# An attention and two-MoE kernel on one core: MoE1's weight differences move from GpSimd to VectorE, each one slot behind its cast, and the first pass of the experts is put in another order

## The chip, the cores and the metric

The kernel runs on one core of a Trainium2 chip, alone. The metric is the device time of one execution in microseconds. Five engines take part: TensorE (PE; its weight loads are shown apart as PEld), VectorE (DVE), ScalarE (ACT), GpSimd (POOL) and SyncE (SP, which here only issues DMAs). Every engine runs its own instructions strictly in order and waits for others through semaphores.

## What is computed

```python
def _moe_ref(x, w_in, w_out):                       # MoE1, dense
    h = x @ w_in                                    # 896x768 @ 768x2048
    g = h * (1.0 / (1.0 + np.exp(-1.702 * h)))
    return (g @ w_out).astype(np.float32)           # 896x2048 @ 2048x768

def _moe2_ref(x, w_gate, w_output_gate, w1, w2):    # MoE2, 8 experts, one per token
    logits = x @ w_gate
    e_idx = np.argmax(logits, axis=1)
    ...                                             # probs = softmax(logits)
    gate_w = probs[np.arange(N), e_idx]
    eom = 1.0 / (1.0 + np.exp(-(x @ w_output_gate)))
    for e in range(E):
        mask = e_idx == e
        h = np.maximum(x[mask] @ w1[e], 0.0)        # 768 -> 1024
        ye = h @ w2[e]                              # 1024 -> 768
        out[mask] = gate_w[mask, None] * eom[mask, e, None] * ye

def reference(**kwargs):
    attn_out = _attn_ref(**attn_kwargs)             # causal attention, 2 x 12 heads x 448 x 64
    x = attn_out.transpose(0, 2, 1, 3).reshape(896, 768)
    return _moe2_ref(x=_moe_ref(x=x, **moe_kwargs), **moe2_kwargs)
```

MoE1's two weight matrices arrive as float64, all else as float32.

## The kernel before

The order of the work is written out by hand: what a line of the program emits goes to the end of its engine's queue, and no scheduler changes that.

**High and low halves.** The dense products run in a fast float32 mode of TensorE that keeps fewer bits. So every operand is split: `hi` is a cast to that mode (ACT), `lo` is the difference between operand and `hi`. A product takes three matmuls: hi·hi, hi·lo, lo·hi.

**The weight stream of MoE1** (class `Stream`, `add64`). There are 48 jobs, one for a tile of 128x512 weights: 24 of `w_in` (keys `i`), 8 and 16 of `w_out` (`oB`, `oA`). A job rebuilds float32 from the float64 words with three VectorE instructions into a buffer `w32` (L219, L221, L224; two buffers), casts it into half 0 of a slot on ScalarE (L226), and puts the difference into half 1 on GpSimd (L228). The generator `work` stops after L221 and after L224 with its cast, so one job takes three steps. `pump(n)` runs n steps where free slots allow it; ring A has 19 slots, ring X three, and a slot comes free when its weights have been used for the last time. `need(key)` runs steps until a tile is there.

**Attention.** 12 pairs of heads, seven query blocks each; scores on PE, maximum on DVE (L379), exponential on ACT, division by the sum on POOL and DVE (L388 to L390), transposes of P on PE (L398), their copies on ACT and DVE (L401), product with V (L416). Two steps of the weight stream are pumped for each pair, in its fourth and its seventh slot.

**MoE1, layer 1.** For f = 0 to 15, 36 matmuls (L437) fill two PSUM tiles of 512 and 384 tokens; then four sigmoids on ACT (L535) and four products on DVE (L536) turn them into a 128-row piece of g. Even f take their PSUM tiles from a ring of three buffers, so the second tile of f+2 takes the buffer of the first tile of f; odd f have a ring of four, two pieces deep. In each f six steps are pumped (twelve from f = 12 on), between the matmuls and ahead of the sigmoids in the queues.

**MoE1, layer 2** (`l2`). First part B (256 output columns) for seven tiles of 128 tokens, then part A (512 columns). The 16 steps over kk come in four units; a unit needs the split of g that `gsplit` made (cast on ACT, L505; difference on DVE, or on POOL for the units that table `GP` lists: 18 of 56). At kk = 5 the previous tile's result y is transposed (`tr_y`, L615) and copied out of PSUM by DVE (`yT`, L617), at kk = 11 the router's product runs on it (L627).

**MoE2.** For each token tile `pick` finds the expert and the weight of a token (L649 to L664), `place` its position in the experts' lists (L670 to L677), and an indirect DMA scatters both into the list in DRAM (L678). An expert's pass (`block`) gathers 128 tokens (`gather`, L686), transposes them (`prep`, L696 to L699), runs 12 weight units, six for each layer, and scatters the result. `split` casts the next unit of expert weights and takes the difference (L300, L301), up to six units ahead; each then issues the load of the same unit two experts on. Pass 0 runs on tokens of the first five tiles, whose list is ready early; during it the last tile is routed, and the list of pass 1 (`le`) and its tokens (`xw`) are fetched: scatter L678, `list_at` L724, `lwin` L790, gather L686, all on POOL's queue, each behind the one before.

## Time and profile before

| | |
|---|---|
| Time, median of 3 runs | 633.17 us (633.08 to 637.72) |
| Profiled execution, its own time | 635.76 us |
| Its span, first to last instruction | 634.0 us |
| Mean granted TensorE clock | 0.978 |
| Busy: PE / DVE / ACT / POOL | 592.1 / 470.1 / 372.1 / 202.4 us |
| DMA | 118.02 MB, 186 GB/s over the span |

The profile shows one execution. "Busy" is the time in which an engine had an instruction in work; a PE instruction's end is modelled, so busy PE time at a lower clock is longer for the same work. In the rows further down, a timeline line has start, duration, engine, line of the kernel, output<-inputs, shape, count, and in brackets the idle time ahead of it with what ended it.

### The profile page before, as it was taken

Reading aid. Unit: us, or ns where it says so; the run is one execution under the profiler, and the core shown is the slowest. Engines: PE = TensorE matmul, PEld = TensorE weight load, DVE = VectorE, ACT = ScalarE, POOL = GpSimd, SP = SyncE. Lnnn points to the kernel's source line nnn. Section 1 sums busy time; section 2 is a strip of 40 time slices with the busy share of each in tenths; the row PEclk is TensorE's granted clock in tenths of the full one; section 3 lists DMA queues with packets and bytes.
Section 4 is the critical chain, followed back from the end, with each engine's and each line's share of the span. In section 5 each row is a group of like instructions: output and inputs, shape, how many; then the busy total and the mean of one; then the engine's idle time right before and its main releaser. Section 6 shows DMA issues by size and latency. Waiting matters only on the chain. (4 is left out here: it accounts for less than half of the span.)

```text
span 634.0 us, 10087 instructions
## 1 busy us (share of the span) xinstructions
PE 592.1 (93%) x3326; PEld 477.9 (75%) x3326; DVE 470.1 (74%) x890; ACT 372.1 (59%) x729; POOL 202.4 (32%) x291
## 2 busy tenths in 40 slices
PE   6999999999999979787999999959999999999995
PEld 4666666688888859687877777747888888888884
DVE  2767877467777786877844457839998888898896
ACT  3888888333333324434332225737888888888885
POOL 3354444334333343757400012230551111011110
PEclk8999999999999979998999999979999999999998
DMA  6835552125444443402592305148999999999950
GB/s 138 244 85 142 115 120 62 55 68 144 135 134 138 140 148 100 150 17 81 162 348 36 131 17 174 53 154 273 353 365 353 360 335 383 380 382 381 382 191 20
DMA packets 93144, 118.02 MB, mean 186 GB/s; under 512 B 40206, under 2 KB 53406, under 8 KB 93088
## 3 DMA queue, kind: packets, MB, share of 16 engines
q1 hardware_dynamic: 88560, 109.05, 53.3%
q0 software_dynamic: 2512, 5.54, 2.5%
q10 hardware_dynamic: 2016, 2.75, 1.2%
q8 instruction: 28, 0.46, 0.4%
q14 instruction: 28, 0.23, 0.1%
HBM read 114.10 MB, written 7.54 MB: 192 GB/s over the span
## 5 line engine op out<-in xcount | busy, mean ns | idle before, releaser
L575 PE MATMUL py<-slotA,gs 128*128 128x256 f32 (+1 forms) x609 | 115.2, 343 | 1.3 <-POOL gs L507 1.3
L575 PEld LDWEIGHTS py<-slotA,gs 128*128 128x128 f32 x609 | 93.4, 196 | 14.4 <-issue 2.7
L437 PE MATMUL ph<-xhi,slotA 128*128 128x512 f32 (+1 forms) x384 | 97.5, 373 | 4.7 <-DVE g L536 4.7
L228 POOL TENSOR_TENSOR slotA<-w,slotA 128x512 fp32r<-128x512 f32 x45 | 62.0, 1379 | 81.7 <-ACT slotA L226 81.6
L437 PEld LDWEIGHTS ph<-xhi,slotA 128*128 128x128 f32 x384 | 70.8, 191 | 15.3 <-issue 5.8
L226 ACT CAST slotA<-w 128x512 fp32r<-128x512 f32 x45 | 27.9, 620 | 89.9 <-DVE w L224 89.9
L301 DVE TENSOR_TENSOR ent<-wraw,ent 128x1024 fp32r<-128x1024 f32 x48 | 58.0, 1221 | 4.9 <-ACT ent L300 4.9
L437 PE MATMUL ph<-xlo,slotA 128*128 128x512 f32 x192 | 56.0, 372 | 0.0
L367 PE MATMUL sc<-kT,qz 128*128 128x64 f32 (+6 forms) x168 | 52.6, 397 | 3.0 <-ACT kT L358 2.8
L507 DVE TENSOR_TENSOR gs<-g,gs 128x512 fp32r<-128x512 f32 x38 | 31.5, 837 | 31.8 <-ACT gs L505 31.8
L390 POOL TENSOR_SCALAR P<-P,rc 128x64 f32<-128x64 f32 (+2 forms) x72 | 36.7, 511 | 54.4 <-DVE rc L389 40.5
L875 PE MATMUL ps_h<-ent,xh 128*128 128x512 f32 x192 | 53.9, 402 | 0.0
L224 DVE SCALAR_TENSOR_TENSOR w<-raw,w 128x512 uint32<-128x512 uint32 x46 | 51.9, 1129 | 1.2
L381 ACT ACTIVATE P<-sc,nmax 128x64 f32<-128x64 f32 (+6 forms) x84 | 40.3, 480 | 18.7 <-DVE nmax L379 7.6
L300 ACT CAST ent<-wraw 128x1024 fp32r<-128x1024 f32 x48 | 49.9, 1051 | 0.4 <-ACT y L597 0.4
L379 DVE TENSOR_REDUCE nmax<-sc 128x1 f32<-128x64 f32 (+6 forms) x84 | 34.6, 416 | 16.6 <-PE sc L368 16.4
L536 DVE TENSOR_TENSOR g<-ph,g 128x256 f32<-128x256 f32 x64 | 23.6, 389 | 30.1 <-ACT g L535 30.1
L505 ACT CAST gs<-g 128x512 fp32r<-128x512 f32 x56 | 33.1, 617 | 14.7 <-PE py L575 9.1
L875 PEld LDWEIGHTS ps_h<-ent,xh 128*128 128x128 f32 x192 | 35.0, 188 | 7.3
L398 PE MATMUL ps_pT<-ident,P 128*128 128x128 f32 x192 | 37.7, 289 | 2.2 <-POOL P L390 1.6
L301 DVE TENSOR_TENSOR ent<-wrb,ent 128x1024 fp32r<-128x1024 f32 x30 | 36.3, 1222 | 4.7 <-ACT ent L300 4.2
L221 DVE SCALAR_TENSOR_TENSOR w<-raw,w 128x512 uint32<-128x512 uint32 x46 | 38.0, 827 | 1.6
(190 smaller groups left out, 1211.8 us busy)
## 6 DMA issues: line engine op xcount, KB each, us to landing
wraw<-in_moe_w_dram SPq DMA_DIRECT2D x66, 512.0 KB, 7.8
wrb<-in_moe_w_dram SPq DMA_DIRECT2D x48, 512.0 KB, 8.2
wr<-in_moe_w_dram SPq DMA_DIRECT2D x30, 512.0 KB, 6.2
raw<-in_moe_w_in_dram SPq DMA_DIRECT2D x24, 512.0 KB, 4.3
raw<-in_moe_w_out_dram SPq DMA_DIRECT2D x22, 512.0 KB, 3.6
qraw<-in_q_dram SPq DMA_DIRECT2D x24, 112.0 KB, 2.9
kraw<-in_k_dram SPq DMA_DIRECT2D x24, 112.0 KB, 2.9
vraw<-in_v_dram SPq DMA_DIRECT2D x24, 96.0 KB, 2.5
```

What stands on the lines that cost most here:

```text
L221: nc.vector.scalar_tensor_tensor(wu, r[:, :, 1], 0xC0000000, wu, op0=ALU.bitwise_and, op1=ALU.bitwise_or)
L224: nc.vector.scalar_tensor_tensor(wu, r[:, :, 0], 29, wu, op0=ALU.logical_shift_right, op1=ALU.bitwise_or)
L228: nc.gpsimd.tensor_sub(slot[:, 1], w, slot[:, 0].bitcast(F32))
L300: nc.scalar.copy(hi, raw)
L301: nc.vector.tensor_sub(lo, raw, hi.bitcast(F32))
L367: nc.tensor.matmul(sc[:, :n], qT[:, j].rearrange("d h p -> d (h p)"), kT[:, :n], start=True, stop=False)
L381: nc.scalar.activation(Pb[j][:, :n], sc[:, :n], AF.Exp, bias=nm, scale=1.0, accum_out=sm)
L390: eng[NORM_ENG[j]].tensor_scalar(Pb[j][:, :n], Pb[j][:, :n], rc, 1.0, op0=ALU.mult, op1=ALU.mult)
L398: nc.tensor.transpose(ps[:, c].rearrange("p h q -> p (h q)"), Pb[j][:, c * KC:(c + 1) * KC], ident)
L437: nc.tensor.matmul(p[:, 0:128 * nt], wt, xt[:, kk, 128 * t0:128 * (t0 + nt)], start=kk == 0 and n == 0, stop=kk == KD - 1 and n == 2)
L575: nc.tensor.matmul(py[:, :n], gt[:, kk % 4], wt, start=kk == 0 and m == 0, stop=kk == KF - 1 and m == 2)
L875: nc.tensor.matmul(hps[hf], xh[:, k0 + n], wt[:, n], start=k0 + n == 0 and m == 0, stop=False)
```

## The change

Five things change.

- **Stream.** The difference of a job (old L228) goes to DVE. It is held back (`st.late`) and emitted in the first step of the next job, between its second and third DVE instruction, or when the tile is needed. A job now takes two steps, not three.
- **gsplit.** All differences of g go to DVE; each is emitted with the next unit's cast.
- **tr_y.** The copy of the transposes goes from DVE to ACT.
- **pick and place of the last tile.** The weight's instructions (`weigh`) stand behind those of the position.
- **Pass 0.** No split in its first three units, two in each of the next three; `prep` stands behind unit 11, not 10; a one-element DMA on SP's queue reads `xw`, so the loads behind it wait for the gather.

```diff
+    def flush(self):
+        if self.late:
+            self.late[1]()
+            self.late = None
+
     def need(self, key):
...
+        if self.late and self.late[0] == key:
+            self.flush()
         return self.slots[key]
...
                 nc.vector.scalar_tensor_tensor(wu, r[:, :, 1], 0xC0000000, wu,
                                                op0=ALU.bitwise_and, op1=ALU.bitwise_or)
+                st.flush()
                 yield
                 nc.vector.scalar_tensor_tensor(wu, r[:, :, 0], 29, wu,
                                                op0=ALU.logical_shift_right, op1=ALU.bitwise_or)
                 nc.scalar.copy(slot[:, 0], w)
-                yield
-                nc.gpsimd.tensor_sub(slot[:, 1], w, slot[:, 0].bitcast(F32))
+                st.late = keys[0], lambda: nc.vector.tensor_sub(slot[:, 1], w, slot[:, 0].bitcast(F32))
...
             nc.scalar.copy(gs[:, 0], src)
-            eng = nc.gpsimd if u in GP else nc.vector
-            eng.tensor_sub(gs[:, 1], src, gs[:, 0].bitcast(F32))
+            while glate:
+                glate.pop()()
+            glate.append(lambda: nc.vector.tensor_sub(gs[:, 1], src, gs[:, 0].bitcast(F32)))
...
-            nc.vector.tensor_copy(yT[:, :n], p[:, :n])
+            nc.scalar.copy(yT[:, :n], p[:, :n])
...
             nc.vector.tensor_copy(pos_i, pos)
+            while late_w:
+                weigh(*late_w.pop())
             nc.gpsimd.indirect_dma_start(
...
-        def block(lw, hooks):
+        def block(lw, hooks, rate=(1,) * NU):
...
-                split()
+                for _ in range(rate[u]):
+                    split()
...
+        gate = dram.tile([1, 1], F32, name="gate")
+
         def first_x():
             gather(le0, xw)
+            nc.sync.dma_start(gate, xw[0:1, 0:1])
 
         block(lw0, {
-            (0, 1): lambda: tr_y(TT - 1, "A"), (0, 2): last_logits, (0, 3): lambda: pick(TT - 1),
+            (0, 1): lambda: tr_y(TT - 1, "A"), (0, 2): last_logits, (0, 3): lambda: pick(TT - 1, True),
             (0, 5): last_place, (1, 0): rest_lists, (1, 3): first_x, (1, 4): counts, 6: further_constants,
-            10: lambda: prep(xw)})
+            11: lambda: prep(xw)}, (0, 0, 0, 2, 2, 2, 1, 1, 1, 1, 1, 1))
```

**VectorE in layer 1 of MoE1.** Before, these rows stand between the last product of piece f = 0 and the first of f = 1 (`ph` are PSUM tiles, `w_...` the buffers `w32`):

```order
L536 TENSOR_TENSOR g_1976<-ph_1916,g_1976 128x128
L219 TENSOR_SCALAR w_2003<-raw 128x512
L221 SCALAR_TENSOR_TENSOR w_2003<-raw,w_2003 128x512
L224 SCALAR_TENSOR_TENSOR w_2003<-raw,w_2003 128x512
L219 TENSOR_SCALAR w_2030<-raw 128x512
L221 SCALAR_TENSOR_TENSOR w_2030<-raw,w_2030 128x512
L224 SCALAR_TENSOR_TENSOR w_2030<-raw,w_2030 128x512
L536 TENSOR_TENSOR g_1973<-ph_1994,g_1973 128x2x128
```

After, these twelve stand in the same place:

```order
L226 TENSOR_SCALAR w_2038<-raw 128x512
L228 SCALAR_TENSOR_TENSOR w_2038<-raw,w_2038 128x512
L235 TENSOR_TENSOR slotA<-w_1979,slotA 128x512
L232 SCALAR_TENSOR_TENSOR w_2038<-raw,w_2038 128x512
L226 TENSOR_SCALAR w_2059<-raw 128x512
L228 SCALAR_TENSOR_TENSOR w_2059<-raw,w_2059 128x512
L235 TENSOR_TENSOR slotA<-w_2038,slotA 128x512
L232 SCALAR_TENSOR_TENSOR w_2059<-raw,w_2059 128x512
L226 TENSOR_SCALAR w_2080<-raw 128x512
L228 SCALAR_TENSOR_TENSOR w_2080<-raw,w_2080 128x512
L235 TENSOR_TENSOR slotA<-w_2059,slotA 128x512
L232 SCALAR_TENSOR_TENSOR w_2080<-raw,w_2080 128x512
```

Two jobs of three instructions have become three jobs of four; the difference L235 is that of the job before. By the order of the rows, the number of jobs ahead of each piece's products was 2 for f = 1 to 11, 4 for f = 12, 3 for f = 13 and 0 for f = 14 and 15; it is now 3 for f = 1 to 4, 1 for f = 5, 3 for f = 7, 8, 11 and 12, and 0 for the others. In the attention 8 jobs are done before and 13 after.

**ScalarE in part B.** Before, the stretch that ends with the copy of the third tile's result (`y`) out of PSUM; `gs` are casts for the split of g, `slotA` those of the stream:

```order
L505 CAST gs<-g_1974 128x512
L226 CAST slotA<-w_3179 128x512
L505 CAST gs<-g_1974 128x512 x3
L226 CAST slotA<-w_3236 128x512
L597 COPY y_3272<-py 128x256
```

After, the stretch that ends with the same copy:

```order
L516 CAST gs<-g_2008 128x512
L234 CAST slotA<-w_3186 128x512
L516 CAST gs<-g_2008 128x512
L629 COPY yT<-ps_yT 128x256
L516 CAST gs<-g_2008 128x512
L234 CAST slotA<-w_3231 128x512
L516 CAST gs<-g_2008 128x512
L234 CAST slotA<-w_3271 128x512
L609 COPY y_3288<-py 128x256
```

A third cast of the stream (one more than before) now stands in this tile, two of them behind the copy of the transposes, the last right ahead of y.

**VectorE while the last tile is routed, in pass 0.** Before, from the negated maximum (L655) to the position as an integer (L677); L301 is the difference of a split:

```order
L655 TENSOR_SCALAR nm<-nm 128x1
L658 TENSOR_TENSOR tmp<-ps_lg,ohb 128x8
L659 TENSOR_REDUCE nm<-tmp 128x1
L661 TENSOR_SCALAR nm<-nm 128x1
L662 TENSOR_SCALAR nm<-nm 128x1
L663 TENSOR_TENSOR nm<-nm 128x1
L664 RECIPROCAL lst<-nm 128x1
L301 TENSOR_TENSOR entb<-wraw,entb 128x1024
L675 TENSOR_TENSOR tmp_4518<-ps_rk,ohb 128x8
L676 TENSOR_REDUCE pos<-tmp_4518 128x1
L677 CAST pos_i<-pos 128x1
```

After, from the same instruction to the first difference of a split:

```order
L667 TENSOR_SCALAR nm<-nm 128x1
L695 TENSOR_TENSOR tmp_4508<-ps_rk,ohb 128x8
L696 TENSOR_REDUCE pos<-tmp_4508 128x1
L697 CAST pos_i<-pos 128x1
L679 TENSOR_TENSOR tmp<-ps_lg,ohb 128x8
L680 TENSOR_REDUCE nm<-tmp 128x1
L682 TENSOR_SCALAR nm<-nm 128x1
L683 TENSOR_SCALAR nm<-nm 128x1
L684 TENSOR_TENSOR nm<-nm 128x1
L685 RECIPROCAL lst<-nm 128x1
L308 TENSOR_TENSOR ent_4343<-wraw,ent_4342 128x1024
```

The position's three instructions (now L695 to L697) stand ahead of the weight's six (now L679 to L685), and the split that stood between them is behind both. Ahead of the hidden layer's second difference (old L892, now L914, its second use) stand the differences of seven splits in this pass, before as after; two of them stood ahead of the position, now none does.

## Rows read from the trace of the kernel before

**Rows 1.** Stretches: length, busy time of each engine, granted clock, DMA.
```profile
122.00:246.86 124.86, 120.12 (x576) 104.83 (x577) 88.92 (x150) 39.44 (x94) 46.12 (x74) 0.97 0.44 128
246.86:307.40 60.54, 50.37 (x382) 46.87 (x382) 47.95 (x54) 25.12 (x50) 40.65 (x28) 0.94 0.27 88
307.40:393.90 86.50, 85.50 (x438) 66.47 (x437) 48.91 (x152) 28.88 (x59) 12.38 (x10) 1.00 0.42 140
393.90:425.00 31.10, 22.47 (x116) 17.77 (x117) 19.71 (x37) 15.60 (x23) 8.74 (x26) 0.90 0.40 126
425.00:634.00 209.00, 201.42 (x1079) 169.83 (x1078) 181.49 (x197) 171.27 (x222) 40.88 (x35) 0.99 0.89 316
```

**Rows 2.** PE's waits: for whom, us in total, times, longest.
```profile
PE ps_lT L627 <- DVE yT L617: 9.1, 7, 3.7
...
PE ph L437 <- DVE g L536: 4.7, 1, 4.7
```

**Rows 3.** Timeline of PE, attention.
```profile
85.13 0.97 PE L416 MATMUL ps_o<-pT,vraw 128*64 128x448 f32 x4 [0.37 <-DVE pT L401]
...
92.73 0.55 PE L398 MATMUL ps_pT<-ident,P 128*128 128x128 f32 x3 [0.27 <-POOL P L390]
```

**Rows 4.** Timeline of DVE, the same pair of heads.
```profile
80.13 0.62 DVE L423 TENSOR_TENSOR xlo<-ps_o,xhi 128x448 fp32r<-128x448 f32 x1 [0.76 <-ACT xhi L422]
```

**Rows 5.** Timeline of DVE, layer 1.
```profile
132.41 0.42 DVE L219 TENSOR_SCALAR w<-raw 128x512 uint32<-128x512 uint32 x1
...
147.47 0.42 DVE L219 TENSOR_SCALAR w<-raw 128x512 uint32<-128x512 uint32 x1
...
148.65 0.69 DVE L224 SCALAR_TENSOR_TENSOR w<-raw,w 128x512 uint32<-128x512 uint32 x1
149.26 0.42 DVE L219 TENSOR_SCALAR w<-raw 128x512 uint32<-128x512 uint32 x1
...
150.44 1.66 DVE L224 SCALAR_TENSOR_TENSOR w<-raw,w 128x512 uint32<-128x512 uint32 x1
...
155.26 0.42 DVE L219 TENSOR_SCALAR w<-raw 128x512 uint32<-128x512 uint32 x1
```

**Rows 6.** Timeline of all engines, end of layer 1 and start of part B.
```profile
228.38 0.38 ACT L535 ACTIVATE g<-ph 128x256 f32<-128x256 f32 x1
...
230.24 0.66 PE L437 MATMUL ph<-xhi,slotA 128*128 128x384 f32 x1 [4.74 <-DVE g L536]
...
244.11 1.29 DVE L507 TENSOR_TENSOR gs<-g,gs 128x512 fp32r<-128x512 f32 x2 [0.21 <-ACT gs L505]
...
246.86 8.07 PE L575 MATMUL py<-slotA,gs 128*128 128x256 f32 x66
```

**Rows 7.** DVE by line, part B: busy us, mean ns, idle before.
```profile
L507 DVE TENSOR_TENSOR gs<-g,gs 128x512 fp32r<-128x512 f32 x11 | 12.5, 1142 | 11.4 <-ACT gs L505 11.3
...
L617 DVE COPY yT<-ps_yT 128x256 f32<-128x256 f32 x6 | 2.5, 415 | 0.0
```

**Rows 8.** POOL by line, part B.
```profile
L507 POOL TENSOR_TENSOR gs<-g,gs 128x512 fp32r<-128x512 f32 x18 | 27.0, 1513 | 12.7 <-ACT gs L505 12.7
```

**Rows 9.** ACT by line, part B.
```profile
L597 ACT COPY y<-py 128x256 f32<-128x256 f32 x7 | 2.6, 366 | 0.2 <-PE py L575 0.2
```

**Rows 10.** Timeline of PE, longest wait of part B.
```profile
295.86 0.60 PE L627 MATMUL ps_lT<-yT,wg 128*32 128x128 f32 x4 [3.66 <-DVE yT L617]
296.39 5.15 PE L575 MATMUL py<-slotA,gs 128*128 128x256 f32 x30
```

**Rows 11.** Timeline of all engines, routing of the last tile and gather.
```profile
396.67 1.22 DVE L301 TENSOR_TENSOR ent<-wraw,ent 128x1024 fp32r<-128x1024 f32 x1
...
402.08 1.23 DVE L301 TENSOR_TENSOR entb<-wraw,entb 128x1024 fp32r<-128x1024 f32 x1 [0.39 <-ACT entb L300]
```

**Rows 12.** The same view, a later window.
```profile
404.04 1.73 POOL L678 DMA_INDIRECT xl_d<-lst,pos_i  x1 [9.80 <-DVE pos_i L677]
...
413.46 1.81 POOL L686 DMA_INDIRECT xw<-y_d,le  x1 [1.22 <-issue]
...
421.10 1.51 PE L696 MATMUL ps_x<-ident,xw 128*128 128x128 f32 x6 [7.51 <-DMA xw<-y_d,le]
...
424.97 1.40 PE L875 MATMUL ps_h<-entb,xh 128*128 128x512 f32 x4
```

**Rows 13.** Gathers of tokens: KB, us from issue to landing.
```profile
xw<-y_d,lw POOLq DMA_INDIRECT x1, 4.6
...
xw<-y_d,le POOLq DMA_INDIRECT x1, 7.5
```

More of the change, by code (lines that the diff above doesn't have):

```diff
@@ L94, in pump @@
                 return
+    def flush(self):
+        if self.late:
+            self.late[1]()
+            self.late = None
     def need(self, key):
@@ L137 @@
     XK = (11, 12, 13)
-    GP = (4, 5, 7, 8, 10, 11, 13, 14, 16, 17, 19, 20, 22, 23, 25, 26, 27, 29)
     R1, R1B = 1, 2
@@ L493 @@
         GU = 4
+        glate = []
         def gsplit(u):
@@ L505, in gsplit @@
             nc.scalar.copy(gs[:, 0], src)
-            eng = nc.gpsimd if u in GP else nc.vector
-            eng.tensor_sub(gs[:, 1], src, gs[:, 0].bitcast(F32))
+            while glate:
+                glate.pop()()
+            glate.append(lambda: nc.vector.tensor_sub(gs[:, 1], src, gs[:, 0].bitcast(F32)))
             gsp[u] = gs
@@ L641, with pick @@
         ohs = {}
-        def pick(t):
+        def pick(t, split_off=False):
             logits_sum(t)
@@ L657, in pick, with weigh @@
                                  accum_out=nm[:, 4:5])
+            if not split_off:
+                weigh(t, nm, tmp, lg, ohb)
+            else:
+                late_w.append((t, nm, tmp, lg, ohb))
+            ohs[t] = ohb
+        late_w = []
+        def weigh(t, nm, tmp, lg, ohb):
             nc.vector.tensor_mul(tmp[:, 2], lg[:, NE:2 * NE], ohb)
@@ L664, in pick @@
             nc.vector.reciprocal(lst[:, t, 1:2], nm[:, 6:7])
-            ohs[t] = ohb
         def place(t):
@@ L926, in block @@
                     nc.scalar.activation(ys[:, 512:768], pyB[:, 0:256], AF.Copy, scale=scl)
-                split()
+                for _ in range(rate[u]):
+                    split()
                 hook(u)
```

## The prediction

> **What bounds the kernel now.** I read the stretches first: what share of each PE works and at which clock. The experts' passes after 425 us are PE at 201.4 of 209.0 us, and the middle of MoE1's second layer (307 to 394 us) at 85.5 of 86.5; nothing is to be had there. Three stretches lose time: layer 1 of MoE1 (120.1 of 124.9 us, granted clock 0.97), part B of layer 2 (50.4 of 60.5, clock 0.94) and pass 0 of the experts (22.5 of 31.1, clock 0.90) [rows 1]. Then PE's waits: in part B PE waits for VectorE's copy of the transposed y (9.1 us in 7 waits), in layer 1 once, 4.7 us, for VectorE's products [rows 2]; in pass 0 for the gathered tokens. So the bound is PE, held up by VectorE's queue in two places and by a chain through DRAM in a third. All sums are made on the profiled execution (635.76 us, span 634.0) and their difference is put on the median, 633.17; the profiled execution lies 2.6 us above that, and I take no account of it.
>
> **Attention.** Each pair's pumps now hold, in the fourth slot, a job's first two instructions with the last job's difference, in the seventh its third one: a whole job for each of 12 pairs where two thirds stood. The pair at 76 to 85 us had these instructions in the same slots, less the difference, and PE then waited 0.37 us for a copy of P; where the first two instructions fell in the seventh slot PE waited 0.27 us [rows 3]. VectorE has a gap of 0.76 us behind the fourth slot [rows 4], as long as the difference that comes in (0.69, as below), so I hide it there. Every pair gets the wait of 0.37 where the mean of the three kinds of pair was about 0.3: **+1 us**. If the gap does not cover it, 12 x 0.69 = +8; POOL, rid of its part, may give back 1.
>
> **Layer 1.** A piece f takes PE 120.1 / 16 = 7.5 us [rows 1]. VectorE's cycle for a piece with two jobs was 155.26 - 147.47 = 7.79 us: one job in 149.26 - 147.47 = 1.79 us, a second whose last instruction took 1.66 us beside POOL's difference where the first's took 0.69, so 2.84 us, and 3.16 us for the last cast, the four sigmoids and products [rows 5]. So VectorE fell 0.3 us behind with every piece, and four jobs at f = 12 then made the wait of 4.74 us: the sigmoids began at 228.38, the first PSUM tile was free 1.86 us later, at 230.24 [rows 6]. PE had stood since 225.50.
>
> Now a job has its difference in VectorE's queue. Two of the same form in a row took 1.29 us [rows 6]; with the first at 0.69, as the job's other two-input instruction alone (148.65, [rows 5]), the next one adds 0.60: 2.39 us a job, none lengthened by POOL, and 3 x 2.39 + 0.1 + 3.16 = 10.4 us for a piece with three jobs. With 0 at the end of f = 0 (128.4, as 13 pieces end at 225.5), VectorE starts the jobs of f = 1 at 132.41 - 128.4 = 4 us [rows 5] and ends the cycles of f = 1 to 4 at 14.4, 24.8, 35.2 and 45.6. The tile that f = 4 needs is free 0.7 us before the second of these, 24.1, and PE is there at 22.6: a wait of 1.5. The one for f = 6 is free at 44.9; PE is there at 37.5 + 1.5 + 0.2 = 39.2: a wait of 5.7. Then the ring is full, only one job follows, and VectorE catches up; the later groups of two pieces with three jobs give under 0.5 each. Some 7.5 to 8 us of waits replace 4.7, and the low clock behind a long wait comes once either way. As the difference also fills the pause between two dependent instructions (0.1 a job), I take **+2 us**, between -3 (jobs held by late slots spread out) and +6 (0.2 us more for each of twelve jobs in the chain, on both waits).
>
> **Part B.** Lost now: 60.5 - 50.4 = 10.2 us of waiting and some 3.6 by the clock (0.06 of the stretch), so 46.7 us would do [rows 1]. VectorE's own waits and lengthened instructions are the cause: 11 differences of g at 1142 ns, where two in a row without POOL took 1.29 us together, with 11.4 us of standing idle for ScalarE's cast just ahead [rows 7], and 18 on POOL at 1513 ns [rows 8]. All of that goes: a difference now comes a slot behind its cast, and POOL does nothing. The copy of y's transposes costs about as much on ScalarE (the copy of y, the same shape out of PSUM, 366 ns [rows 9]) as on VectorE (415 [rows 7]); there it no longer stands behind a job's three instructions, which made the wait of 3.66 us [rows 10].
>
> What is late next: VectorE's queue, bunched. Ten jobs at 2.39 and 29 differences at 0.65, with 3 us of small things, are 46 us, against PE's 46.7, but eight of the jobs fall into the first four tiles. A tile costs PE 48 matmuls of 8.07 / 66 = 0.122 us [rows 6], 5.9 us, and about 0.8 for transposes and logits; in the third tile, with three jobs, VectorE needs 3 x 2.39 + 4 x 0.62 = 9.7. Followed from the first tile on, VectorE is 3 to 4 us behind at the end of the third, where ScalarE's copy of y stands behind the third job's cast: the transposes of that y then wait about 2.7 us. The first tile's fourth unit waits 1.1 us for a difference behind a job, the others together 1.4. After the wait of 3.66 us PE ran at the lower clock: 30 matmuls took 5.15 us [rows 10], 0.17 each, 1.5 us too much; I count 1.3 once. So 46.7 + 5.2 + 1.3 = 53.2: **-7.3 us**, between 0 (below) and -12.5.
>
> A rule speaks against this part. The trace shows POOL's difference lengthening VectorE's instruction by 1.66 - 0.69 = 0.97 us [rows 5]; moved, it costs VectorE 0.60. The Trainium skill (Perfetto Trace Analysis, Optimizing Scalar/DVE Operations) says that GpSimd and VectorE share a read port into SBUF, so that shifting operations between these two may not help. By that rule the term is near 0 and the sum 629.8; by the rows each move gives VectorE 0.4 us back, and the idle time ahead of it besides.
>
> **Part A and pass 0.** Part A is PE at work; the copy on ScalarE saves it some 0.5 us of waits at the last tiles: **-0.5**.
>
> In pass 0 PE came to the transposes of the tokens at 421.10 - 7.51 = 413.6 and began pass 1 at 424.97 [rows 12], 11.4 us for 2.4 us of work. The chain: the position's scatter at 404.04, list, gather issued at 413.46 [rows 12], landing 7.5 us later; the earlier gather, with no loads beside it, took 4.6 [rows 13]. A split of 1.23 us stood ahead of the position, one of 1.22 ahead of the router's sum [rows 11]; both now stand behind. So the scatter goes 1.2 us earlier at least (1.7 with what the second delays), and as the loads now wait for the gather, 413.46 - 1.2 + 4.6 = 416.9 is when the tokens are there. What is late next: the splits. Seven differences of 1.22 and the hidden layer's two (0.7 each) stand in a row from about 403.5 on, so the second hidden half is ready at 413.4; unit 9 waits for it, then units 9 to 11 run until 417.2, with the tokens there already. Transposes and casts, which unit 11 no longer covers, take 2.2 us: 419.4 instead of 424.97, and 0.3 us of low clock less: **-5.9**, between -2 and -8. The loads held back by the added DMA on SP's queue start some 5 us later; a unit's place is needed two passes (over 30 us) after its load is issued, so nobody waits.
>
> **The sum.** +1 + 2 - 7.3 - 0.5 - 5.9 = -10.7: 633.2 - 10.7 = **622.5 us**, with 617 to 627 as this case's own range.
>
> **The rivals.**
> 1. *VectorE is not late.* With jobs held up by slots or loads, layer 1 waits 3 us and part B 1: 4.5 and 5.5 us less, 612.5. For it: idle VectorE in part B vanishes. Against: the counted rows of its queue. Chance 0.20.
> 2. *The exchange of engines gives nothing in part B*, since PE waits for VectorE's queue there and that gets more instructions: 622.5 + 7.3 = 629.8. For it: 46 us of VectorE against 46.7 of PE, in bunches. Against: what it has now is 48 us of lengthened work and 11 of standing idle [rows 1, 7]. Chance 0.13. (It is where the rule quoted above would lead.)
> 3. *Pass 0 trades one wait for another*: the seven splits, ScalarE's casts ahead of them and the uncovered casts of the tokens take back all but 2 us: 626.4. Chance 0.12.
> 4. *Slower: a difference costs VectorE 1.14 us there too*, as in rows 7, because something other than POOL lengthens it. A job takes 2.93 us and a piece with three 12.0; layer 1 waits some 17 us (+12), the attention's gap no longer covers it (12 x 0.4 = +5), part B needs 10 x 2.93 + 29 x 1.1 + 3 = 64 us (+4): +12 + 5 + 4 - 0.5 - 5.9 = 647.8. It decides from about 0.9 us on. Against it: the pair at 244.11, where no POOL instruction ran. Chance 0.05.
>
> **How the numbers follow.** The forecast has 0.50. One per cent, 6.3 us, is about what a measurement of this kernel tells from no change; the bound of faster is 626.8. Below it lie nearly all of the forecast, rival 1 and over half of rival 3: 0.77. Rival 2 and the rest of 3 make 0.18 of no change, rival 4 0.05. The range, 612 to 629, leaves out rival 4, most of 2 and the better half of 1.
>
> **What would show it.** In part B no wait for the copy of y's transposes, VectorE's differences all near 0.69 us, one wait for y itself in the fourth tile. In layer 1 the long wait at f = 6 instead of f = 14. In pass 0 a gather of under 5 us and pass 1 six microseconds earlier against the end of part A. I am wrong if the attention gets longer by more than 3 us, or if layer 1's waits go over 10.

## The result and the profile after

The changed kernel takes **625.98 us** (median, 625.63 to 626.22), the kernel before on the same chip 633.78 (633.08 to 637.72). The ratio is 0.9853, with an interval of 0.982 to 0.9885. The profiled execution after took 625.63 us, its span is 623.5 us, against 635.76 and 634.0 before.

The stretches of the changed kernel (columns as in [rows 1]; cut at the stages' bounds, which are defined below; the cuts of [rows 1] lie within 0.2 us of the same places, save its first, which is 1.0 us later):

```profile
124.89:251.99 127.10, 121.47 (x581) 105.38 (x582) 81.82 (x166) 37.73 (x90) 2.60 (x22) 0.97 0.38 110
251.99:303.75 51.76, 47.11 (x382) 44.09 (x381) 44.91 (x83) 28.28 (x57) 0.74 (x1) 1.00 0.38 118
303.75:389.79 86.04, 85.80 (x441) 66.46 (x439) 40.86 (x141) 32.02 (x65) 9.21 (x8) 1.00 0.40 131
389.79:413.39 23.60, 20.76 (x116) 15.99 (x116) 18.40 (x36) 16.73 (x26) 8.61 (x27) 1.00 0.28 87
413.39:623.50 210.11, 201.44 (x1078) 169.59 (x1078) 182.04 (x199) 170.34 (x221) 39.81 (x35) 0.99 0.91 323
```

For a comparison by stage: each stage ends where PE begins the first product of the next (the attention where the 448-wide product of its last pair begins). In us, from the two profiled executions:

| stage | before | after | difference | predicted |
|---|---|---|---|---|
| attention, up to its last product | 120.97 | 124.89 | +3.9 | +1 |
| layer 1 | 125.89 | 127.10 | +1.2 | +2 |
| part B | 60.39 | 51.76 | -8.6 | -7.3 |
| part A | 86.67 | 86.04 | -0.6 | -0.5 |
| pass 0 | 31.05 | 23.60 | -7.4 | -5.9 |
| the passes behind | 209.03 | 210.11 | +1.1 | 0 |
| sum | 634.0 | 623.5 | -10.5 | -10.7 |

Part B and pass 0 now run at the full granted clock, 1.00 where [rows 1] have 0.94 and 0.90. PE is at work 47.1 of 51.8 us in part B. Layer 1 keeps its clock of 0.97, and PE is idle for 5.6 us in it, where it was 4.7.

PE's waits after (for whom, us in total, times, longest), which answer to [rows 2]:

```profile
PE ph L444 <- DVE g L548: 5.6, 2, 5.0
PE ps_o L423 <- DVE pT L408: 3.7, 9, 0.4
...
PE ps_yT L627 <- ACT y L609: 2.2, 2, 1.8
...
PE ps_lT L639 <- ACT yT L629: 0.6, 2, 0.4
```

The 9.1 us for the copy of the transposes have become 0.6, behind ScalarE. (These are waits of the whole run; 8.1 of the 9.1 lay in part B.) The wait for `ph` went from 4.7 in one to 5.6 in two. The second row is the attention's: nine pairs with 0.4 us each, where there were three. The same row before, and in a run described below that does the differences on POOL in the same slots:

```profile
PE ps_o L416 <- DVE pT L401: 1.1, 3, 0.4
```
```profile
PE ps_o L424 <- DVE pT L409: 2.9, 8, 0.4
```

That run has eight of these waits and its attention ends at 121.1 us, as before. So they are not what makes the attention 3.9 us longer.

PE's timeline in layer 1 and part B, the waits alone:

```profile
155.63 0.41 PE L444 MATMUL ph<-xhi,slotA 128*128 128x384 f32 x1 [0.61 <-DVE g L548]
...
175.76 0.66 PE L444 MATMUL ph<-xhi,slotA 128*128 128x384 f32 x1 [5.02 <-DVE g L548]
```
```profile
257.67 3.62 PE L587 MATMUL py<-slotA,gs 128*128 128x256 f32 x28 [0.97 <-DVE gs L519]
...
271.67 0.41 PE L639 MATMUL ps_lT<-yT,wg 128*32 128x128 f32 x4 [0.44 <-ACT yT L629]
...
277.68 0.44 PE L627 MATMUL ps_yT<-ident,y 128*128 128x128 f32 x2 [1.81 <-ACT y L609]
...
284.82 0.44 PE L627 MATMUL ps_yT<-ident,y 128*128 128x128 f32 x2 [0.42 <-ACT y L609]
```

These are the predicted places: 0.61 us at f = 4 (predicted 1.5), 5.02 at f = 6 (5.7), a first wait for a difference (0.97, predicted 1.1), and the wait for y itself in the fourth tile, 1.81 (2.7). VectorE's differences, which answer to [rows 7] (1142 ns, 11.4 us of idle ahead of them):

```profile
L519 DVE TENSOR_TENSOR gs<-g,gs 128x512 fp32r<-128x512 f32 x30 | 20.1, 683 | 2.1 <-ACT gs L516 2.1
```

Thirty of them at 683 ns. The chain of pass 0, which answers to [rows 12]:

```profile
397.72 0.98 POOL L700 DMA_INDIRECT xl_d<-lst,pos_i  x1 [6.92 <-DVE lst L685]
...
406.29 1.87 POOL L708 DMA_INDIRECT xw<-y_d,le  x1 [1.97 <-PE ps_yB L923]
...
407.88 0.73 PE L923 MATMUL ps_yA<-ent,hl 128*128 128x512 f32 x2 [1.20 <-DVE hl L914]
...
411.24 0.82 PE L718 MATMUL ps_x<-ident,xw 128*128 128x128 f32 x6
...
413.39 1.19 PE L897 MATMUL ps_h<-entb,xh 128*128 128x512 f32 x4 [1.33 <-ACT xh L720]
```

The scatter is issued 7.9 us after the pass begins (10.1 before), the gather lands 4.7 us after its issue, and PE goes straight on to the transposes at 411.24 without a wait for it. Its longer waits are 1.20 us for the hidden layer's difference and, at the end, 1.33 us for the cast of the tokens.

### The profile page after: what moved, and what is told of

Read it like the earlier page. It is cut to its first block, busy times and chain, and to the rows that moved or that the text cites. A ratio compares the mean times of both kernels' runs of the same rounds, so it can differ in the third digit from the quotient of the medians.

```text
span 623.5 us, 10060 instructions
## 1 busy us (share of the span) xinstructions
PE 590.3 (95%) x3326; PEld 473.6 (76%) x3326; DVE 463.9 (74%) x942; ACT 376.9 (60%) x743; POOL 106.7 (17%) x225
## 5 line engine op out<-in xcount | busy, mean ns | idle before, releaser
L587 PE MATMUL py<-slotA,gs 128*128 128x256 f32 (+1 forms) x609 | 112.5, 337 | 1.0 <-DVE gs L519 1.0
L587 PEld LDWEIGHTS py<-slotA,gs 128*128 128x128 f32 x609 | 90.8, 190 | 13.6 <-issue 2.6
L548 DVE TENSOR_TENSOR g<-ph,g 128x256 f32<-128x256 f32 x64 | 23.6, 389 | 41.5 <-ACT g L547 41.5
L519 DVE TENSOR_TENSOR gs<-g,gs 128x512 fp32r<-128x512 f32 x56 | 37.5, 683 | 16.6 <-ACT gs L516 16.6
L386 DVE TENSOR_REDUCE nmax<-sc 128x1 f32<-128x64 f32 (+6 forms) x84 | 34.4, 411 | 10.7 <-PE sc L375 10.7
L547 ACT ACTIVATE g<-ph 128x256 f32<-128x256 f32 x64 | 20.9, 355 | 33.5 <-PE ph L444 17.2
L444 PEld LDWEIGHTS ph<-xlo,slotA 128*128 128x128 f32 x192 | 35.8, 192 | 4.6
L228 DVE SCALAR_TENSOR_TENSOR w<-raw,w 128x512 uint32<-128x512 uint32 x46 | 35.0, 762 | 1.6
```

The source lines that it names most:

```text
L228: nc.vector.scalar_tensor_tensor(wu, r[:, :, 1], 0xC0000000, wu, op0=ALU.bitwise_and, op1=ALU.bitwise_or)
L386: nc.vector.tensor_reduce(nm, sc[:, :n], axis=AX.X, op=ALU.max, negate=True)
L444: nc.tensor.matmul(p[:, 0:128 * nt], wt, xt[:, kk, 128 * t0:128 * (t0 + nt)], start=kk == 0 and n == 0, stop=kk == KD - 1 and n == 2)
L519: glate.append(lambda: nc.vector.tensor_sub(gs[:, 1], src, gs[:, 0].bitcast(F32)))
L587: nc.tensor.matmul(py[:, :n], gt[:, kk % 4], wt, start=kk == 0 and m == 0, stop=kk == KF - 1 and m == 2)
```

## The experiments

Each ran beside the kernel before on the same chip, on four chips in all; the kernel before took 633.2 to 634.0 us in every set. Times are medians, ratios are against the kernel before. Stages are cut as above, from each kernel's profile.

| kernel | attention | layer 1 | part B | part A | pass 0 | rest | median us | ratio (interval) |
|---|---|---|---|---|---|---|---|---|
| pass 0 alone | 120.7 | 125.9 | 60.4 | 86.6 | 23.7 | 209.3 | 629.10 | 0.9944 (0.9924 to 0.9964) |
| g alone | 120.9 | 125.9 | 47.9 | 86.4 | 28.8 | 209.7 | 621.40 | 0.9816 (0.9773 to 0.9858) |
| g and y's copy | 121.5 | 125.3 | 47.5 | 86.0 | 29.1 | 209.6 | 621.98 | 0.983 (0.9797 to 0.9862) |
| stream alone | 125.0 | 127.2 | 61.1 | 86.5 | 28.7 | 209.9 | 640.88 | 1.0126 (1.0105 to 1.0147) |
| changed, all on POOL | 121.1 | 130.6 | 60.4 | 86.0 | 23.6 | 210.0 | 634.42 | 1.0008 (0.9989 to 1.0027) |
| changed, old stream | 121.0 | 125.9 | 47.5 | 86.3 | 23.6 | 209.1 | 615.02 | 0.971 (0.968 to 0.9741) |
| old stream, g on POOL | 121.4 | 125.2 | 58.3 | 86.0 | 23.6 | 209.7 | 626.37 | 0.9886 (0.9864 to 0.9907) |
| two thirds of the pace | 131.8 | 119.0 | 48.2 | 86.2 | 23.6 | 209.7 | 619.88 | 0.9776 (0.9739 to 0.9812) |
| the same, first loads early | 124.1 | 125.2 | 48.2 | 86.2 | 23.6 | 210.0 | 619.57 | 0.9777 (0.9758 to 0.9797) |
| old stream, slower last quarter | 121.0 | 120.5 | 48.2 | 87.3 | 23.6 | 209.2 | 613.02 | 0.9676 (0.9655 to 0.9698) |
| changed, no wait on SP | 125.2 | 127.8 | 51.8 | 86.1 | 23.6 | 210.1 | 626.21 | 0.9877 (0.9841 to 0.9914) |
| changed, even splits | 124.7 | 127.6 | 51.8 | 86.1 | 25.5 | 210.0 | 627.47 | 0.9898 (0.9875 to 0.9921) |

### The parts one by one

**Pass 0 alone**: the kernel before with the diff's `pick`, `weigh`, `place`, `block` and `first_x`.

> The kernel before with the change of pass 0 alone: the weight's instructions behind the position's, splits in the order 0 0 0 2 2 2 1 1 1 1 1 1, the preparation of the second pass behind the last step, and the wait on SP's queue for the gather. Theory: pass 0 goes from 31.05 to 23 to 24.5 us as in the changed kernel and all else stays (the loads that SP holds back are not late, since the passes behind have their weights long before), total 626 to 627 us. Rival (the passes behind lose what pass 0 gains, since SP's loads stand still for 20 us): pass 0 24 us and the passes behind 213 us or longer, total 630 us.

Pass 0 took 23.7 us, all else stood, and the passes behind took 209.3: the held loads cost nothing. The time, 629.1 us, is 4.1 under before (the theory had 626 to 627) and not the 7 that the profiles' pass 0 suggests. The likely reason is the profiled execution of before: its pass 0 took 31.05 us with a gather of 7.5 us, while three other kernels with the old pass 0 took 28.7, 28.8 and 29.1 with gathers of 6.3, 6.0 and 5.8. (There is no second profile of before that would show it.) The part is worth 4 to 5 us: 4.1 by the medians, 5.0 to 5.4 against those three.

**The stream alone**: the kernel before with the diff's `flush` and `work`.

> The kernel before with the change of the weight stream alone: two steps for a job in place of three, its difference on VectorE behind the next job's first two instructions. g's differences, the copy of y's transposes and pass 0 are those of before. Theory: the attention and layer 1 lose as in the changed kernel (attention ends at 124.9 us, was 121.0; layer 1 takes 127.1 us, was 125.9), part B gains only what the stream's share of POOL's work is worth there (it goes from 60.4 to 56 to 59 us), pass 0 stays at 31 us; total 634 to 638 us, so not faster than before. Rival (the stream's differences on POOL are what slows VectorE in part B): part B at 52 to 54 us and a total of 630 us.

It is 7.7 us slower than before, more than I expected: the attention loses 4.0, layer 1 1.3, and part B gains nothing (61.1), where the theory had 56 to 59 and the rival less. PE now waits there 6.9 us for ScalarE's copy of y (0.8 before) and 4.3 for VectorE's copy of its transposes (8.1 before). This third of the change is a loss.

**g and the copy**: the kernel before with the diff's `gsplit` and `tr_y`.

> The kernel before with g's differences all on VectorE, one slot behind their cast, and with the copy of y's transposes on ScalarE; the stream keeps its three steps and POOL, pass 0 is that of before. Theory: the attention and layer 1 are as before (121.0 us, 125.9 us with its wait of 4.7 us), part B goes from 60.4 to 52 to 56 us, since 18 of the differences that ran beside VectorE are gone and 9 to 12 of the stream stay; pass 0 31 us; total 627 to 631 us. Rival (VectorE was late by its own work, and more of it makes it later): part B 60 us or longer, total 634 us or more.

Part B fell to 47.5 us, below the expected range and 4.3 us below the changed kernel's 51.8, with the stream's differences still on POOL. Together the three parts make +7.7 - 11.2 - 4.1 = -7.6 us; the whole change measured -7.8. g's part carries the change. That the totals agree does not mean that the parts add up: in part B g's part makes -12.9 us and the stream's +0.7, which would be -12.2, and the whole change made -8.6.

**g alone**: the same without the copy of y's transposes.

> The kernel before with g's differences all on VectorE, one slot behind their cast, and nothing else: the copy of y's transposes stays on VectorE, the stream and pass 0 are those of before. Theory (18 of g's differences leaving POOL is nearly the whole gain of part B): part B 48 to 51 us, with waits for the copy of 0.3 to 0.6 us each in place of the 9.1 us of before, total 622 to 626 us. Rival (the copy behind VectorE's queue is the wait that ends last, and moving it is the gain): part B 55 us or longer, total 628 us or more.

Part B 47.9, so the copy on ScalarE is worth some 0.5 us of it, and nothing that the total shows (621.4 without it, 622.0 with it). The waits of 9.1 us for that copy in [rows 2] were VectorE's queue, not the copy's place.

### Which engine does the differences

**The changed kernel with its differences on POOL.**

```diff
-                st.late = keys[0], lambda: nc.vector.tensor_sub(slot[:, 1], w, slot[:, 0].bitcast(F32))
+                st.late = keys[0], lambda: nc.gpsimd.tensor_sub(slot[:, 1], w, slot[:, 0].bitcast(F32))
-            glate.append(lambda: nc.vector.tensor_sub(gs[:, 1], src, gs[:, 0].bitcast(F32)))
+            glate.append(lambda: (nc.gpsimd if u in GP else nc.vector).tensor_sub(gs[:, 1], src, gs[:, 0].bitcast(F32)))
```

> The changed kernel with MoE1's differences put back on POOL: all of the stream's, and the 18 of the 56 of g that stood there before; the slots in which they are emitted, the copy of y's transposes on ScalarE and the whole of pass 0 stay as changed. Theory (the gain of part B is that POOL no longer works beside VectorE, and the loss of the attention is the difference in VectorE's queue): part B goes back from 51.8 to 57 to 60 us, the end of the attention from 124.9 to 121 to 122 us, pass 0 stays at 23.6 us; total 629 to 632 us. Rival 1 (part B gains by the emission one slot later and by the copy on ScalarE, whatever engine does the difference): part B stays at 51 to 53 us. Rival 2 (the attention loses by the added jobs, one for each pair of heads where there were two for three, and not by the engine of the difference): the attention still ends at 124 to 125 us. With both rivals the total is 626 us.

Part B is back at 60.4 us (the theory had 57 to 60) and the attention at 121.1, as the theory had it. Against the changed kernel the attention differs in the engine of the stream's difference alone, so that engine costs it 3.8 us. The total of 634.4 lies above its range because layer 1 took 130.6: three jobs a piece with POOL beside them made waits of 2.7, 4.5, 0.7 and 0.4 us for `ph`. In part B VectorE's instructions are long again; its and POOL's groups there (busy us, mean ns, idle ahead):

```profile
L520 DVE TENSOR_TENSOR gs<-g,gs 128x512 fp32r<-128x512 f32 x12 | 16.0, 1339 | 5.0 <-ACT gs L517 5.0
L229 DVE SCALAR_TENSOR_TENSOR w<-raw,w 128x512 uint32<-128x512 uint32 x9 | 12.1, 1345 | 0.3
L233 DVE SCALAR_TENSOR_TENSOR w<-raw,w 128x512 uint32<-128x512 uint32 x8 | 9.3, 1159 | 0.1
```
```profile
L520 POOL TENSOR_TENSOR gs<-g,gs 128x512 fp32r<-128x512 f32 x18 | 28.2, 1578 | 6.4 <-ACT gs L517 6.4
```

**The changed kernel with the old stream, and the same with 18 of g's differences on POOL.** The first restores this (the second has the second pair of lines above besides):

```diff
-                st.flush()
                 yield
...
-                st.late = keys[0], lambda: nc.vector.tensor_sub(slot[:, 1], w, slot[:, 0].bitcast(F32))
+                yield
+                nc.gpsimd.tensor_sub(slot[:, 1], w, slot[:, 0].bitcast(F32))
```

> The changed kernel with the weight stream of before: three steps for a job, its difference on POOL in a step of its own. g's differences stay on VectorE, one slot behind their cast, y's transposes are copied on ScalarE, pass 0 stays as changed. Theory (the parts add up, the stream's part is the loss): attention ends at 121 to 122 us, layer 1 takes 125 to 126 us, part B 47.5 us, pass 0 23.7 us, total 617 to 619 us, below the changed kernel by 7 to 9 us. Rival (the stream on POOL was cheap in part B only because pass 0 and the loads stood as before, or one gain covers the other): 621 to 625 us.

> The changed kernel with the weight stream of before and with the 18 differences of g back on POOL that stood there before; they are still emitted one slot behind their cast, y's transposes are still copied on ScalarE, and pass 0 stays as changed. Against the run with the stream of before (part B 47.5 us, 615.0 us) only the engine of those 18 differs. Theory (VectorE's instructions are lengthened by the POOL instruction beside them, and that made part B late): part B 56 to 60.5 us, VectorE's difference of g at a mean of over 1.0 us there, total 624 to 628 us. Rival (the later slot and the copy on ScalarE take the waits out, whatever engine it is): part B 48 to 51 us, total 615 to 618 us.

615.0 and 626.4 us, part B 47.5 and 58.3. The first lies below the range of its theory, 617 to 619: without the stream's part the changed kernel gains 11.0 us, where that part alone cost 7.7. Of these, 4.3 are part B's (51.8 to 47.5). So the stream on VectorE costs more once g's differences are there too. Between the two runs only the engine of 18 differences changes, so it is that engine, and not the later slot or the copy, that most of part B's gain comes from (10.8 of 12.9 us). In the second run PE waits in part B 2.7 us for POOL's differences themselves and 6.5 us for VectorE's and for ScalarE's copies of y and of its transposes; in the first 0.6 in all. So POOL's own slowness has a share beside VectorE's lengthened instructions. VectorE's differences of g in part B, first with all of them on VectorE, then with 18 on POOL:

```profile
L519 DVE TENSOR_TENSOR gs<-g,gs 128x512 fp32r<-128x512 f32 x30 | 24.2, 817 | 3.4 <-ACT gs L516 3.4
```
```profile
L520 DVE TENSOR_TENSOR gs<-g,gs 128x512 fp32r<-128x512 f32 x12 | 14.5, 1218 | 7.0 <-ACT gs L517 7.0
```

817 ns are not the 683 of the changed kernel, since the stream's nine differences on POOL still lengthen some; yet this part B is shorter. With VectorE not full (43.1 of 47.5 us), that costs PE next to nothing: PE is at work 46.8 of the 47.5 us.

### The pace of the stream

**Two thirds of the credits**, so that a job of two steps comes as often as one of three did; and the same with a first credit that issues the first loads as early as before.

```diff
-        self.credit += n
+        self.credit += n * 2 / 3
```
```diff
         self.late = None
+        self.credit = 0.34
```

> The changed kernel with each credit of the stream multiplied by two thirds, so that a job of two steps comes as often as one of three steps did before (two jobs for three pairs of heads, two for a piece of layer 1, two thirds as many in part B); the difference stays on VectorE. Theory 1 (the stream on VectorE loses because its jobs come one and a half times as often): attention ends at 121 to 122 us, layer 1 takes 123 to 126 us with no wait of 5 us at its seventh piece, part B 47 to 50 us, total 616 to 620 us. Theory 2 (it loses because each difference takes 0.6 us of VectorE's queue wherever that is full): attention 123 to 124.5 us, layer 1 as before, part B 50 to 52 us, total 621 to 625 us.

> The kernel of the run with two thirds of the stream's credits, with a third of a credit to begin with, so that the stream's first loads are issued at 16 us again, in place of 27 us, and VectorE doesn't stand 5.0 us for the first of them in the attention; its difference stays on VectorE. Theory (that wait and what it brought, 131.8 us in place of 121 to 123 us at the end of the attention, was the first loads' alone, and a job that comes as often as before makes the stream on VectorE harmless): attention ends at 121.5 to 123 us, layer 1 119 to 121 us without a wait for PSUM of over 1 us, part B 48 us, total 610 to 613 us, below the kernel with the stream of before (615.0 us). Rival (the engine and not the pace costs the attention): attention ends at 124 us or later, total 613.5 us or more.

The first run was disturbed by my edit: the first loads came ten microseconds later and VectorE stood for them, so its attention is no evidence. In the second that is gone, and the attention still ends at 124.1 us: the rival holds, the engine costs the attention 3 us at the old pace too (121.0 with the old stream), though the slots of the jobs are not quite the same there. Part B is 48.2 in both, 3.5 us less than in the changed kernel: there it is the pace that costs, with nine jobs in place of eleven. Of the 11.0 us between 626.0 and 615.0 some 6.4 go with the pace (619.6) and 4.6 with the engine. VectorE and PE in a pair of heads of the second run:

```profile
64.38 0.50 DVE L227 TENSOR_SCALAR w<-raw 128x512 uint32<-128x512 uint32 x1
...
64.92 0.69 DVE L229 SCALAR_TENSOR_TENSOR w<-raw,w 128x512 uint32<-128x512 uint32 x1
...
65.53 0.68 DVE L236 TENSOR_TENSOR slotA<-w,slotA 128x512 fp32r<-128x512 f32 x1
...
66.13 0.22 DVE L387 TENSOR_REDUCE nmax<-sc 128x1 f32<-128x64 f32 x1
...
67.41 0.55 PE L406 MATMUL ps_pT<-ident,P 128*128 128x128 f32 x3 [1.08 <-POOL P L398]
```

The three instructions of the stream hold VectorE from 64.38 to 66.13; the maximum of a 64-wide score block stands behind them, and PE waits 1.08 us for the P that comes out of that chain. It is so in one pair of three. (Layer 1 kept one wait there, 4.4 us, at piece 14.)

**The old stream with one step in place of two** behind each product of the last quarter of layer 1.

```diff
-    R1, R1B = 1, 2
+    R1, R1B = 1, 1
```

> The changed kernel with the weight stream of before, as in the run that had that, and with one step of the stream in place of two behind each product of the last quarter of layer 1. Theory (the wait of 4.8 us at piece 14 comes of the four jobs in piece 12, each of 2.75 us of VectorE beside the difference on POOL): the wait goes, layer 1 takes 119 to 121 us, part B stays at 47.5 to 49 us with two or three jobs more, total 608.5 to 611 us. Rival (the jobs that are put off are missed in part B or part A): layer 1 119 to 121 us and parts B and A longer by 3 us or more together, total 613 to 616 us.

613.0 us, the lowest median here, but only 2.0 us below the run with two steps and in the rival's range, not in the theory's. Layer 1 took 120.5 us with no wait for `ph` left, as the theory has it; parts A and B together took 1.8 us more, which is some of the rival. What the wait was made of stands in the kernel with two steps (615.0 us); VectorE's stretch, the first difference on POOL in it, and PE behind it:

```profile
218.86 0.69 DVE L231 SCALAR_TENSOR_TENSOR w<-raw,w 128x512 uint32<-128x512 uint32 x1
...
220.65 1.67 DVE L231 SCALAR_TENSOR_TENSOR w<-raw,w 128x512 uint32<-128x512 uint32 x1
...
223.41 1.67 DVE L231 SCALAR_TENSOR_TENSOR w<-raw,w 128x512 uint32<-128x512 uint32 x1
...
226.18 1.63 DVE L231 SCALAR_TENSOR_TENSOR w<-raw,w 128x512 uint32<-128x512 uint32 x1
228.84 0.42 DVE L548 TENSOR_TENSOR g<-ph,g 128x256 f32<-128x256 f32 x1 [1.02 <-ACT g L547]
```
```profile
220.34 1.43 POOL L235 TENSOR_TENSOR slotA<-w,slotA 128x512 fp32r<-128x512 f32 x1 [3.79 <-ACT slotA L233]
```
```profile
230.28 0.66 PE L444 MATMUL ph<-xhi,slotA 128*128 128x384 f32 x1 [4.76 <-DVE g L548]
```

The same instruction takes 0.69 us while POOL stands (it had been idle for 3.79 us at 220.34) and 1.63 to 1.67 beside the difference on POOL. One job of 1.8 us, three of 2.8 and 3.2 us of products make 13.3 us, more than the 7.5 us that PE needs for a piece.

### The parts of pass 0

**Without the transfer on SP's queue that waits for the gather.**

```diff
         def first_x():
             gather(le0, xw)
-            nc.sync.dma_start(gate, xw[0:1, 0:1])
```

> The changed kernel without the small transfer on SP's queue that waits for the gather of pass 1, so that loads go on beside it. Theory (the gather takes 4.2 to 4.7 us with nothing beside it and 5.8 to 7.5 us with loads beside it, and nothing stands between it and the second pass): the gather lands 1 to 3 us later and pass 0 takes 24.5 to 27 us, total 627 to 629 us. Rival (the gather is now issued so early that its landing no longer counts, and the wait costs loads): pass 0 23.6 us or less, total 625 to 626 us.

No change: 626.2 us, pass 0 23.6, and the gather landed in 4.2 us. My theory falls. POOL and SP in that pass:

```profile
399.18 0.98 POOL L700 DMA_INDIRECT xl_d<-lst,pos_i  x1 [7.38 <-DVE lst L685]
...
407.74 1.45 POOL L708 DMA_INDIRECT xw<-y_d,le  x1 [1.25 <-PE ps_yA L921]
...
410.02 4.34 SPq L279 DMA_DIRECT2D wr<-in_moe_w_dram  x4
```

SP has no load to issue before 410.02; the gather at 407.74 is ahead of the loads by itself. In the kernel before, four loads were issued from 412.09 on, ahead of the gather at 413.46 [rows 12]:

```profile
412.09 4.81 SPq L272 DMA_DIRECT2D wr<-in_moe_w_dram  x4
```

Counted from the pass's begin, the loads come 19.2 us in (18.2 before), since the splits whose buffers they refill come later, and the gather 16.9 (19.5 before). So it is chiefly the earlier gather that puts it ahead.

**One split a step**, with all else of pass 0 as changed.

```diff
-            11: lambda: prep(xw)}, (0, 0, 0, 2, 2, 2, 1, 1, 1, 1, 1, 1))
+            11: lambda: prep(xw)})
```

> The changed kernel with one split for each step of pass 0 again, in place of 0 0 0 2 2 2 1 1 1 1 1 1; the weight's instructions stay behind the position's, the preparation of pass 1 at the last step, and SP still holds its loads behind the gather. Theory (the splits that stood ahead of the last tile's position are the gain of pass 0): the scatter is issued 2 to 4 us later than in the changed kernel (after pass 0's begin: 9 to 12 us, was 7.9 us), the gather too, and pass 0 takes 25.5 to 28 us, total 628 to 630 us. Rival (the weight's six instructions and the later preparation are the gain): pass 0 23.6 to 24.5 us, total 626 us.

Pass 0 took 25.5 us, and the scatter was issued 11.5 us after the pass began, where the changed kernel has 7.9. So the order of the splits is worth 1.9 of some 5 us. The scatter is even later than before (10.1 us), and the gather's issue, at 19.3 us, is where it was (19.5); yet it landed by 414.4, 4.8 us after its issue, with the loads behind it. So what is left of the gain here lies behind the gather's issue: in its landing without loads ahead of it, for which in this order the wait on SP may well be needed, and in the later preparation. The weight's instructions bring nothing by themselves, and the changed kernel's rows show why: the scatter carries position and weight, and now waits for the weight (`lst`, above), which is ready 1.1 us after the position:

```profile
396.20 0.15 DVE L697 CAST pos_i<-pos 128x1 int32<-128x1 f32 x1
...
397.28 0.16 DVE L685 RECIPROCAL lst<-nm 128x1 f32<-128x1 f32 x1
```

I did not part the wait from the preparation.

## Why the prediction was right, and where it was off

The time came out 3.5 us above the forecast of 622.5 and inside its own range. The mechanisms of part B, layer 1 and pass 0 were those of the forecast. In the attention the forecast's own sign of being wrong came true: more than 3 us longer, and it was 3.9. That the sum of terms (-10.7) met the difference of the two profiles (-10.5) is luck: the steps are off by +2.9 and +1.1 on one side and by -0.8, -1.3, -0.1 and -1.5 on the other. By its steps:

- **Part B, -7.3, measured -8.6.** The reason holds for g: VectorE's instructions were lengthened by POOL's beside them, and g's differences leaving POOL brought 10.8 us (58.3 to 47.5) with all else the same. Right too: next to no wait for the copy (0.6 us in two), differences at 0.68, one longer wait for y in the fourth tile. What I had not parted is g from the stream: the stream's move and faster pace take back 4.3 us of part B. Rival 2, that the exchange of engines gives nothing, is false for g and true for the stream. The move pays for the 18 differences of g, which took 27 us of POOL in part B, and not for the stream's nine (part B 47.5 us with them on POOL, 48.2 on VectorE at the same pace). The Trainium skill (Perfetto Trace Analysis, Optimizing Scalar/DVE Operations) warns that GpSimd and VectorE share a read port into SBUF, so that a move between them may not help. The trace agrees that POOL's work slows VectorE's (0.69 against 1.67 us); that the port is the cause, no run here shows.
- **Attention, +1, measured +3.9.** This is the step that failed, in its overlap: "VectorE has a gap of 0.76 us behind the fourth slot [rows 4], as long as the difference that comes in (0.69, as below), so I hide it there". The gap is a wait for ScalarE's cast of the product, later in the same chain; it moved along with the chain. With the same jobs in the same slots it is 0.53 us with the difference ahead of it and 0.51 us without. VectorE in a pair of the changed kernel, and in the one with the differences on POOL:

```profile
78.64 0.41 DVE L226 TENSOR_SCALAR w<-raw 128x512 uint32<-128x512 uint32 x1
79.09 1.01 DVE L228 SCALAR_TENSOR_TENSOR w<-raw,w 128x512 uint32<-128x512 uint32 x1
80.02 0.68 DVE L235 TENSOR_TENSOR slotA<-w,slotA 128x512 fp32r<-128x512 f32 x1
80.62 0.28 DVE L386 TENSOR_REDUCE nmax<-sc 128x1 f32<-128x128 f32 x1
...
82.69 0.62 DVE L430 TENSOR_TENSOR xlo<-ps_o,xhi 128x448 fp32r<-128x448 f32 x1 [0.53 <-ACT xhi L429]
```
```profile
76.35 0.41 DVE L227 TENSOR_SCALAR w<-raw 128x512 uint32<-128x512 uint32 x1
76.79 1.01 DVE L229 SCALAR_TENSOR_TENSOR w<-raw,w 128x512 uint32<-128x512 uint32 x1
77.72 0.28 DVE L387 TENSOR_REDUCE nmax<-sc 128x1 f32<-128x128 f32 x1
...
79.98 0.62 DVE L431 TENSOR_TENSOR xlo<-ps_o,xhi 128x448 fp32r<-128x448 f32 x1 [0.51 <-ACT xhi L430]
```

The difference puts the next maximum 0.6 us back (1.98 us after the job's first instruction in place of 1.37), and PE's pair takes 9.47 us in place of 9.08. PE's listed wait for `ps_o` is 0.42 us in place of 0.36 in these pairs, so the rest is spread over delays too short for a row. The jobs, one for each pair in both kernels, cost nothing by themselves: 121.1 us against 121.0 before. The bound that I gave, +8 if the gap covers nothing, was the right kind of term; about half of it came.

- **Layer 1, +2, measured +1.2**, with the long wait at f = 6 (5.02 us, predicted 5.7) and a shorter one at f = 4 (0.61, predicted 1.5).
- **Part A and pass 0, -0.5 and -5.9, measured -0.6 and -7.4.** The second is 4 to 5 us by the run of pass 0 alone. The chain is the predicted one, but quicker: the scatter went 2.2 us earlier (predicted 1.2 to 1.7), the gather 3.0 (predicted 1.2), and the tokens were there 21.2 us after the pass began (predicted 23.0). The hidden layer's difference is the wait that is left (1.20 us), and transposes and casts took the predicted 2.2 us. The held loads, which I gave as the reason for the short gather, are not needed. And the earlier gather of [rows 13] was not one "with no loads beside it": SP issued five from 1.6 us behind it on.

```profile
386.52 1.70 POOL L686 DMA_INDIRECT xw<-y_d,lw  x1 [1.76 <-DMA lw<-xl_d]
...
388.09 5.37 SPq L272 DMA_DIRECT2D wraw<-in_moe_w_dram  x5
```

- **The base.** "The profiled execution lies 2.6 us above that, and I take no account of it": some 2 us of that most likely lay in the very stage that I sized, in one slow gather (31.05 us against 28.7 to 29.1 in the three other kernels with the old pass 0). The sum of terms missed the difference of the medians (-7.8) by 2.9 us, mostly by this.
- The passes behind became 1.1 us longer, which no term had. Kernels with the old pass 0 or the old stream also took 209.1 to 209.9; what makes the rest is open.

The changed kernel thus holds a gain by g, the copy and pass 0 (15.3 us as the sum of the two runs, 18.4 in the run that has them together) and a loss by the stream, 7.7 us alone and 11.0 between 626.0 and 615.0. With the stream left as it was, and its pace in the last quarter halved, the kernel takes 613.0 us.

## What to carry to other kernels

When one edit moves the same operation in several places, size each place by itself: here the move paid where POOL's share was large and VectorE's queue had idle time between lengthened instructions, and cost where VectorE's queue was already on the path from one matmul to the next. An idle gap covers new work only if the work comes behind the instruction that the gap waits for; ask what the gap waits for before spending it. Totals that add up do not show that the parts do: compare them stage by stage. And where the profiled execution lies above the median, look for the stage that holds the excess before that stage's saving is counted in full.

## What the runs showed of the hardware

- A difference on POOL (1.3 to 1.7 us for 128x512) lengthened VectorE's two-input instructions beside it from 0.69 to 1.63 to 1.67 us, and its one-input ones as well (L226, a shift and mask: 417 ns in part B of the changed kernel; its counterpart L219 931 ns before).
- Back to back on VectorE such a difference costs 0.60 us, less than its length of 0.68 to 0.69 (80.02 to 80.62 above).
- The gather of pass 1 landed in 3.8 to 4.8 us in the nine profiles where no load was issued ahead of it and its landing is recorded, and in 5.8, 6.0, 6.3 and 7.5 us in the four where loads of 512 KB were issued with it or ahead of it.
- The gather of pass 0 had loads issued behind it in all 14 profiles. It landed in 3.6 to 4.6 us in the seven where the first load was issued 1.3 to 2.1 us after it, and in 5.8 to 6.2 us in the seven where that was 1.0 to 1.25 us. What makes this difference is open; in the slower seven POOL's own instruction for the gather lasted longer too (1.8 to 2.1 us in place of 1.1 to 1.7).
